# Last full group of 1024 tokens in a fused attention and soft-MoE kernel: its tokens and exponentials turned by TensorE, its slot sums placed behind the last attention sums

## The chip, the core and the metric

The kernel runs on one core of one Trainium2 chip. The metric is the device time of one execution in microseconds (us). The median of three runs of the kernel before is 1390.17 us (1388.31 to 1393.09).

## The reference

An attention without softmax is followed by a soft mixture of experts over all tokens of all batches. B is 8, S is 2496, D is 256, the key width is 64, N = B * S = 19968 tokens, 8 experts with 4 slots each make 32 slots, and F is 1024.

```python
scores = (1 / S) * z @ z.T                    # per batch
x = u * (maximum(scores, 0) ** 2 @ v)         # [N, D], all batches in a row
logits = x @ phi                              # [N, 32]
d = exp(logits - logits.max(0)); d /= d.sum(0) + 1e-9     # over the tokens
slot_input = d.T @ x                          # [32, D]: the slot sums
slot_out = per expert: maximum(slot_input @ w1, 0) @ w2
c = exp(logits - logits.max(1)); c /= c.sum(1) + 1e-9     # over the slots
out = c @ slot_out                            # [N, D]
```

## The kernel before

**Attention.** For each batch the queries go in chunks of up to 512, and for each chunk the 20 key tiles of 128 go in ten *halves* of two tiles. A half needs its squared scores: they are made by TensorE and ScalarE (`scores`, the two activations in `prepare`) or, where the mirrored block was already made, loaded from a turned copy in DRAM (`fetch`, DMA r<-turned). `prepare` splits them into a rounded part `ph` (a cast, mostly by ScalarE) and a rest `pl` (VectorE), and the sums over the keys (PE acc<-ph,v and acc<-pl,v, 12 matmuls for a half of full shape) need both. Past the first dozen halves `prepare(k)` is called three halves ahead of the sums that use it; when a half's scores are made anew, it stands in the middle of the sums of the half three earlier. `ph`, `pl` and `r` have four buffers each, so a cast waits for the sums of four halves earlier. The last chunk of the last batch is cut into two chunks of 256 queries: these are the last twenty halves, here numbered 0 to 19.

**Soft MoE of a group.** When a chunk's sums end, VectorE multiplies them with u into `xg_q`, which holds x of 1024 tokens, turned (features on partitions). `groups(q)` returns a list of small steps, and the main loop takes one step from the list `work` ahead of each half's sums (in the last twenty halves at every half). The steps are: `logits` (TensorE, then VectorE for the running maximum), `exps` (ScalarE), the turning of x and of the exponentials so that tokens lie on partitions, the slot sums (TensorE), adding them to `slot_acc` (`add_up`, VectorE), and the softmax over the slots (`combine`, `combine_exp`, `combine_sum`, `combine_turn`). The lists `middle` and `behind` hold functions that the next `prepare` runs, between its two activations and at its end.

**The turning.** VectorE transposes 32 by 32 blocks (`turn_block` four times, `turn_e` once) into `y`, and `shift` moves the blocks of `y` to their partitions of `xt` with four DMAs each (xt<-y); there are four shifts for a group, 16 DMAs. All DMAs are issued by SyncE (SP), in the order of the program. An instruction there that waits holds up all that follow: the loads of r, of u and of the expert weights w.

**Slot sums.** For a group before the last two, `slot_sums` is run inside the `logits` of the next group. For group 18, the last full one (tokens 18432 to 19455, its second half finished by the chunk that ends just ahead of half 0), there is a schedule of its own in the else branch of `groups`. In the kernel before, two turning steps are taken ahead of the others, `logits` stands at half 5, the shifts at halves 8 to 11, `combine` and its followers at 12 to 15, `slot_sums` at half 16 and `add_up` at 17. The slot sums write the one buffer of the PSUM pool `ms_ps`.

**The tail.** The last 512 tokens (group 19) are treated after the loop: x is multiplied, `logits` of the last group, `exp`, two of the four x tiles turned by TensorE (`turn_x`, tr_last and et_sums; the other two were turned ahead of halves 18 and 19, tr_first), the slot sums of that group (et_sums<-xt), merging of the two maxima, then the expert layers (h, hT, po) and the output (`tokens`: pf by TensorE, ot by ScalarE and VectorE, the store outT by DMA). Ahead of its `logits` stand four transposes without use (`fill(4)`). The weights w of the experts are loaded during the last thirty halves and just behind the loop, into buffers that the attention frees.

Of the kernel before, what the change touches and what calls it, by code (L numbers as in the profile page):

```python
# [8 lines left out]
F32 = mybir.dt.float32  # L9
# [3 lines left out]
ALU = mybir.AluOpType  # L13
# [3 lines left out]
P = 128  # L17
B, S, D, DQK = 8, 2496, 256, 64
N = B * S
E_, SE, FF = 8, 4, 1024  # L20
NS = E_ * SE
# [5 lines left out]
NQG = (NG + 1) // 2  # L27
# [4 lines left out]
NRAW = 4  # L32
# [32 lines left out]
def attn_soft_moe_kernel(ctx, tc, uT, v, zz, phi, ww, outT):  # L65
    nc = tc.nc

    pe, act, dve, sp = (InOrder(tc, x) for x in (nc.tensor, nc.scalar, nc.vector, nc.sync))
# [10 lines left out]
    ms_ps = ms_st.enter_context(tc.tile_pool(name="ms_ps", bufs=1, space=PSUM, side="right"))  # L79
# [3 lines left out]
    raws = moe.enter_context(tc.tile_pool(name="raws", bufs=1))  # L83
# [47 lines left out]
    for p in range(NP):  # L131
        two = [(load_v, 2 * p), (load_v, 2 * p + 1)]
# [13 lines left out]
    ident = cpool.tile([P, P], F32, name="ident")  # L146
# [8 lines left out]
    xt = xpool.tile([P, 4, NB], F32, name="xt")  # L155
    slot_acc = [cpool.tile([P, D + 1], F32, name=f"slot_acc{i}") for i in range(2)]
# [70 lines left out]
    middle, behind, stores = [], [], []  # L227
# [181 lines left out]
    def finish_chunk(b, ch, acc):  # L409
        _, _, n, t0 = ch  # L410
        ut = ut_.pop(t0)
        s = 0
        while s < n:
            q, o = divmod(t0 + s, 1024)
            w = min(n - s, 1024 - o)
            if q not in xg_:
                xg_[q] = wk.tile([P, 2, 1024], F32, tag="xg", name=f"xg_{q}")
            for c in (slice(0, 1), slice(1, 2)) if t0 + n == N else (slice(0, 2),):
                dve.tensor_mul(xg_[q][:, c, o : o + w], acc[:, c, s : s + w], ut[:, c, s : s + w])
            if o + w == 1024:  # L420
                work.extend(todo_.pop(q, None) or groups(q))
            elif q == NQG - 2 and o + w == 512:

                todo_[q] = groups(q)
                work.extend([todo_[q].pop(0) for _ in range(2)])
            s += w

    late, adding, todo_ = [], [], {}


    xt_last = [xt[:, t, 0:D] for t in range(4)]
# [6 lines left out]
    def copy_x(copy, ps, t):  # L438
        copy(
            xt_last[t].rearrange("p (g c f) -> p c g f", c=2, f=32),  # L440
            ps.rearrange("p (c g f) -> p c g f", c=2, f=32),
        )

    def shift(src, a):


        for b in range(4):
            sp.dma_start(xt[32 * b : 32 * b + 32, a], src[32 * a : 32 * a + 32, b])

    def groups(q):  # L450
# [81 lines left out]
        def slot_sums(ps):  # L532
            for j in range(2):
                for t in range(4):
                    o = 2 * D + j * NS
                    for h, rows in enumerate(HALF):
                        pe.matmul(
                            ps[t * NS : (t + 1) * NS, h, 0:D].rearrange("p (g n) -> p g n", g=4),
                            xt[rows, t, o : o + NS],
                            xt[rows, :, j * D + t * 64 : j * D + (t + 1) * 64],  # L540
                            start=(j == 0), stop=(j == 1),
                        )
            (behind if q < NQG - 3 else adding).append(lambda: add_up(ps))

        def add_up(ps):
# [12 lines left out]
            dve.tensor_add(snew[:, 0:D], snew[:, 0:D], ps[:, 1, 0:D])  # L558

        blocks = [lambda j=j, c=c: behind.append(lambda: turn_block(j, c)) for j in range(2) for c in range(2)]  # L560
        shifts = [lambda a=a: shift(y(), a) for a in range(4)]
        e, c0, c2, c3 = (lambda f=f: behind.append(f) for f in (turn_e, combine, combine_sum, combine_turn))
        ex, c1 = (lambda f=f: middle.append(f) for f in (exps, combine_exp))
        rest = lambda: None
        if q < NQG - 2:

            todo = [logits, ex, *blocks, e, shifts[0], c0, shifts[1], c1, shifts[2], c2, shifts[3]]
            todo.append(lambda: (c3(), late.append(slot_sums)))
        else:


            add = lambda: behind.append(adding.pop(0))
            todo = [*blocks[:2], rest, *blocks[2:], rest, logits, ex, e, lambda: (shifts[0](), add()), *shifts[1:]]
            todo += [c0, c1, c2, c3]
            todo.append(lambda: slot_sums(ms_ps.tile([P, 2, 512], F32, tag="ms", name=f"sl_{q}")))
            todo.append(add)
        return todo

    parts = {}
# [50 lines left out]
    work = []  # L630
# [43 lines left out]
    def between_last(k):  # L674

        if k:
            if k == 1:
                xps.append(sc_ps.tile([P, 2, QC], F32, tag="sc", name="tr_first"))
            ps = xps[0][:, k - 1, 0:D]
            turn_x(ps, xg_[NQG - 1], k - 1)  # L680
            copy_x(act.copy, ps, k - 1)

# [22 lines left out]
    for h, x in enumerate(halves):  # L705
# [23 lines left out]
        if x.ends:  # L729
            finish_chunk(x.b, x.ch, acc)  # L730
# [16 lines left out]
    q = NQG - 1  # L747
    x = xg_.pop(q)
    mold, sold = runmax[(q + 1) % 2], slot_acc[(q + 1) % 2]
# [3 lines left out]
    snew = tiny[:, 512 : 512 + D + 1]  # L753
# [6 lines left out]
    E = wk.tile([P, 2 * P], F32, tag="E", name="E_last", bufs=1)[:, 0:P]  # L760
# [18 lines left out]
    def fill(n, ps=ep_):  # L779
# [18 lines left out]
    for t, copy, ps in (2, act.copy, xq[:, 0, 0:D]), (3, dve.tensor_copy, ep_[:, 1, 0:D]):  # L798
        turn_x(ps, x, t)
        copy_x(copy, ps, t)  # L800
# [234 lines left out]
```

## Time and profile before

| | |
|---|---|
| median of three runs | 1390.17 us |
| profiled execution, its time | 1389.86 us |
| span of the profiled execution | 1387.9 us |
| time outside the span (start and end) | 1.96 us |
| TensorE (PE) busy | 1355.0 us, 98% of the span |
| VectorE (DVE) busy | 1083.1 us, 78% |
| ScalarE (ACT) busy | 913.2 us, 66% |
| mean granted TensorE clock | 0.982 |

The profile is of one execution. Its page gives busy times, the span in 40 slices, the chain of work that ended last and the costliest groups of instructions; the trace behind it answers questions on a stretch of time (timeline by engine, windows, waits). Times in the trace are us from the start of the span. Nearly all instructions carry line 61, that of a helper that keeps each engine's program order, so rows are told apart by the names of their tiles: `out<-in`. A row "[5.80 <-DMA xt<-y]" says that the engine sat idle 5.80 us ahead of it, until that transfer ended. Rows of matmuls give lengths that overlap, since matmuls are pipelined; the chain of work gives steps that add up.

### The profile page before, as it was taken

To read this page: it belongs to the slowest core of one execution; us is meant where nothing else is said; L and a number is where in the kernel's file an instruction comes from. 1 tells how busy PE (TensorE), PEld (TensorE's weight loads), DVE (VectorE), ACT (ScalarE), POOL (GpSimd) and SP (SyncE) were. 2 spreads that over 40 slices of the span, in tenths; PEclk is the share of its full clock that TensorE was granted. 3 is DMA by queue.
4 is the path that set the end of the run, shared out by engine and by line. 5 is a ranking of instruction groups with operands and counts; after the bars stand their busy time and mean duration, and the time that the engine had idled before them with its cause. 6 is when DMAs were issued, how large, how long until landed. Compare 5 with 4: busy or idle time off the path is not lost.

```text
span 1387.9 us, 27271 instructions
## 1 busy us (share of the span) xinstructions
PE 1355.0 (98%) x11029; PEld 1074.4 (77%) x11029; DVE 1083.1 (78%) x1401; ACT 913.2 (66%) x1046; POOL 4.2 (0%) x22
## 2 busy tenths in 40 slices
PE   9999999999999999999999999999999999999785
PEld 6777887788777887778877888778877788778652
DVE  6868896779878798579977888687986979676454
ACT  7866786657756687556857677466866677664253
POOL 0000000000000000000000000000000000000000
PEclk9999999999999999999999999999999999999985
DMA  4336567394676747576665755758565856659889
GB/s 130 78 106 184 192 156 198 99 302 149 167 210 213 254 108 184 154 233 211 175 197 137 291 147 135 208 166 292 130 175 167 296 163 166 199 173 330 265 333 387
DMA packets 106493, 272.74 MB, mean 197 GB/s; under 512 B 14720, under 2 KB 17280, under 8 KB 95104
## 3 DMA queue, kind: packets, MB, share of 16 engines
q1 hardware_dynamic: 106368, 271.02, 64.2%
q8 instruction: 86, 1.41, 0.4%
q14 instruction: 39, 0.32, 0.1%
HBM read 148.41 MB, written 100.14 MB: 179 GB/s over the span
## 4 chain that ended last, share of the span: by engine, by line
PE 91%; DMA 3%; ACT 2%; DVE 2%; SPq 1%; issue 1%; ACTq 0%; DVEq 0%
PE acc L61 72%; PE sc L61 12%; PE lg L61 2%; DMA r<-turned 2%; PE pf L61 2%; ACT ot L61 1%; DMA xt<-y 1%; SPq L61 1%; DVE pl L61 1%; PE po L61 1%; ACT r L61 1%; PE h L61 1%; DMA ut<-in_uT 0%; PE idle L61 0%; DVE y L61 0%
## 5 line engine op out<-in xcount | busy, mean ns | idle before, releaser
L61 PE MATMUL acc<-ph,v 64*128 64x512 f32 (+5 forms) x5092 | 986.2, 386 | 0.4 <-DVE v L61 0.4
L61 PEld LDWEIGHTS acc<-ph,v 64*128 64x128 f32 (+1 forms) x5092 | 598.5, 185 | 147.4 <-issue 20.0
L61 DVE TENSOR_TENSOR pl<-r,ph 128x1024 fp32r<-128x1024 f32 (+1 forms) x412 | 487.3, 1189 | 186.5 <-ACT ph L61 172.0
L61 PE MATMUL acc<-pl,v 64*128 64x512 f32 (+5 forms) x2546 | 623.4, 383 | 1.3 <-DVE pl L61 1.1
L61 ACT CAST ph<-r 128x1024 fp32r<-128x1024 f32 (+1 forms) x259 | 261.6, 1021 | 196.8 <-DMA r<-turned 132.3
L61 ACT ACTIVATE r<-sc 128x1024 f32<-128x1024 f32 (+1 forms) x252 | 255.1, 1013 | 188.2 <-PE sc L61 179.4
L61 PEld LDWEIGHTS acc<-pl,v 64*128 64x128 f32 (+1 forms) x2546 | 307.5, 185 | 62.3 <-DVE pl L61 3.9
L61 ACT ACTIVATE r<-r 128x1024 f32<-128x1024 f32 (+1 forms) x252 | 263.5, 1047 | 7.2
L61 DVE STREAM_TRANSPOSE y<-r 128x1024 f32<-128x1024 f32 x152 | 188.2, 1238 | 0.0
L61 PE MATMUL sc<-z,z 64*128 64x512 f32 x960 | 138.6, 393 | 0.9 <-ACT r L61 0.9
L61 DVE CAST ph<-r 128x1024 fp32r<-128x1024 f32 (+1 forms) x153 | 102.0, 667 | 42.2 <-ACT r L61 40.7
L61 PEld LDWEIGHTS sc<-z,z 64*128 64x128 f32 x960 | 89.7, 184 | 23.4 <-ACT r L61 2.2
L61 PE MATMUL sc<-z 64*128 64x512 f32 (+1 forms) x480 | 67.7, 387 | 0.0
L61 DVE TENSOR_TENSOR xg<-acc,ut 128x1024 f32<-128x1024 f32 (+7 forms) x57 | 48.3, 869 | 20.0 <-PE acc L61 20.0
L61 DVE TENSOR_TENSOR v<-vr,v 128x512 fp32r<-128x512 f32 x80 | 54.0, 674 | 3.6 <-ACT v L61 3.6
L61 DVE STREAM_TRANSPOSE y<-xg 128x512 f32<-128x512 f32 x76 | 52.5, 691 | 0.0
L61 PEld LDWEIGHTS sc<-z 64*128 64x128 f32 x480 | 44.4, 184 | 8.7
L61 ACT CAST v<-vr 128x512 fp32r<-128x512 f32 x80 | 48.7, 609 | 2.1 <-DMA vr<-in_v 2.1
L61 DVE TENSOR_TENSOR z<-zr,z 64x512 fp32r<-64x512 f32 x70 | 48.1, 687 | 2.0
L61 ACT CAST z<-zr 64x512 fp32r<-64x512 f32 x70 | 43.4, 620 | 2.0 <-DMA zr<-in_zz 0.3
L61 DVE COPY ot<-pf 128x1024 f32<-128x1024 f32 (+2 forms) x22 | 24.3, 1104 | 21.6 <-PE pf L61 21.6
L61 ACT COPY ot<-pf 128x1024 f32<-128x1024 f32 (+2 forms) x22 | 20.1, 916 | 25.6 <-PE pf L61 25.6
(128 smaller groups left out, 408.1 us busy)
## 6 DMA issues: line engine op xcount, KB each, us to landing
turned<-y SPq DMA_DIRECT2D x304, 256.0 KB, 4.3
r<-turned SPq DMA_DIRECT2D x72, 1024.0 KB, 7.8
xt<-y SPq DMA_DIRECT2D x304, 72.0 KB, 3.4
vr<-in_v SPq DMA_DIRECT2D x80, 256.0 KB, 2.9
w<-in_w SPq DMA_DIRECT2D x32, 512.0 KB, 7.5
outT<-ot SPq DMA_DIRECT2D x16, 1024.0 KB, 6.5
ut<-in_uT SPq DMA_DIRECT2D x31, 512.0 KB, 4.3
zr<-in_zz SPq DMA_DIRECT2D x35, 256.0 KB, 7.7
```

Of the source, the lines that this page charges most:

```text
L61: return lambda *a, **k: self.tc.keep_in_program_order(f(*a, **k))
```

## The change

The change concerns group 18, and what of the tail stands next to it.

- `turn_block`, `turn_e`, the 16 DMAs xt<-y and the early start of two steps are gone for this group; `logits` now stands at half 2, `exps` at 3, the adding of group 17's slot sums at 4, a new `add_counts` (one small VectorE instruction) at 5, and `combine` and its followers at halves 6 to 9.
- At half 10 TensorE turns the exponentials (two transposes, `turn_e_whole`) and ScalarE copies them into `xt`. At halves 11 to 14 TensorE turns x, four transposes at each (`turn_x_whole`), and ScalarE copies each of these with two instructions. All of them go through the one buffer of `ms_ps`.
- The slot sums (`last_slot_sums`) are put on the list `late` and run behind the loop, ahead of the `logits` of the tail, as 8 matmuls over all 128 tokens of a tile instead of 16 over 64 each. One VectorE instruction adds them to `slot_acc`.
- In the tail `fill(4)` is gone; `fill(2)`, which stays, writes a tile of its own; the turned tiles of the last 512 tokens lie in two buffers of the pool `raws` and no longer in `xt`.

```diff
-                work.extend(todo_.pop(q, None) or groups(q))
-            elif q == NQG - 2 and o + w == 512:
-                todo_[q] = groups(q)
-                work.extend([todo_[q].pop(0) for _ in range(2)])
+                work.extend(groups(q))
...
+        def turn_e_whole():
+            ps = ms_ps.tile([P, 2, 512], F32, tag="ms", name=f"et_{q}")
+            for j in range(2):
+                pe.transpose(ps[:, 0, j * P : (j + 1) * P], E()[:, j * P : (j + 1) * P], ident)
+            act.copy(
+                xt[:, :, 2 * D :].rearrange("k t (j s) -> k j t s", s=NS),
+                ps[:, 0, 0 : 2 * P].rearrange("k (j t s) -> k j t s", j=2, s=NS),
+            )
+
+        def turn_x_whole(i):
+            j, t0 = i // 2, i % 2 * 2
+            ps = ms_ps.tile([P, 2, 512], F32, tag="ms", name=f"xt_{q}_{i}")
+            for k in range(2):
+                turn_x(ps[:, k], x, 4 * j + t0 + k)
+            for k in range(2):
+                copy_x(act.copy, ps[:, k, 0:D], xt[:, t0 + k, j * D : (j + 1) * D])
+
+        def last_slot_sums(ps):
+            for j in range(2):
+                for t in range(4):
+                    pe.matmul(
+                        ps[t * NS : (t + 1) * NS, 0, 0:D], xt[:, t, 2 * D + j * NS : 2 * D + (j + 1) * NS],
+                        xt[:, t, j * D : (j + 1) * D], start=(j == 0), stop=(j == 1),
+                    )
+            snew, sold = slot_acc[q % 2], slot_acc[(q + 1) % 2]
+            dve.scalar_tensor_tensor(
+                snew[:, 0:D], sold[:, 0:D], m[:, 3:4], ps[:, 0, 0:D], op0=ALU.mult, op1=ALU.add
+            )
...
-            add = lambda: behind.append(adding.pop(0))
-            todo = [*blocks[:2], rest, *blocks[2:], rest, logits, ex, e, lambda: (shifts[0](), add()), *shifts[1:]]
-            todo += [c0, c1, c2, c3]
-            todo.append(lambda: slot_sums(ms_ps.tile([P, 2, 512], F32, tag="ms", name=f"sl_{q}")))
-            todo.append(add)
+            todo = [rest, rest, logits, ex, lambda: behind.append(adding.pop(0)), lambda: behind.append(add_counts)]
+            todo += [c0, c1, c2, c3, turn_e_whole, *[lambda i=i: turn_x_whole(i) for i in range(4)]]
+            todo.append(lambda: late.append(last_slot_sums))
...
+    late.pop()(ms_ps.tile([P, 2, 512], F32, tag="ms", name="sl_last"))
+
     acc_st.close()
     sc_st.close()
...
-    xq = ms_ps.tile([P, 2, 512], F32, tag="ms", name="tr_last")
+    xq = tp[:, 1, 0:D]
...
-    fill(4)
     logits(0)
     logits(1)
...
-    fill(2, xq)
+    fill(2)
```

On TensorE, at the end of the last sums and the start of the tail, the kernel before has these rows (acc are the sums of half 19, et_sums<-ident the transposes without use, lg_last the logits of the last 512 tokens, the last two the turning of their tiles 2 and 3):

```order
L61 MATMUL acc_15110<-pl_15270,v_5_12649 128x256
L61 MATMUL et_sums<-ident 128x128 x4
L61 MATMUL lg_last<-xg_15108,phi_sb 32x128 x8
L61 MATMUL tr_last<-ident,xg_15108 128x128 x2
L61 MATMUL et_sums<-ident,xg_15108 128x128 x2
```

The changed kernel has at the same place:

```order
L61 MATMUL acc_15106<-pl_15264,v_5_12649 128x256
L61 MATMUL sl_last<-xt 32x256 x8
L61 MATMUL lg_last<-xg_15104,phi_sb 32x128 x8
L61 MATMUL et_last<-ident,xg_15104 128x128 x2
L61 MATMUL et_sums<-ident,xg_15104 128x128 x2
```

The slot sums of group 18 (sl_last) have taken the place of the four transposes without use; before, they stood ahead of the sums of half 16.

On ScalarE, around halves 7 to 13, the kernel before has these rows (ph_15022 to ph_15195 are the casts for halves 10, 11, 14, 15 and 16, r_15082 and r_15126 the two activations each for halves 12 and 13, L the exponentials of the softmax over the slots):

```order
L61 CAST ph_15022<-r_14867 128x2x256
L61 CAST ph_15044<-r_14867 128x2x256
L61 ACTIVATE r_15082<-sc_15083 128x2x256
L61 ACTIVATE r_15082<-r_15082 128x2x256
L61 ACTIVATE r_15126<-sc_15127 128x2x256
L61 ACTIVATE r_15126<-r_15126 128x2x256
L61 CAST ph_15155<-r_15019 128x2x256
L61 CAST ph_15174<-r_15019 128x2x256
L61 ACTIVATE L_14937<-L_14937 128x256
L61 CAST ph_15195<-r_15063 128x2x256
```

The changed kernel has there (casts for halves 10, 11, 14 and 15, activations for 12 and 13):

```order
L61 ACTIVATE L_14880<-L_14880 128x256
L61 CAST ph_15025<-r_14903 128x2x256
L61 CAST ph_15042<-r_14903 128x2x256
L61 ACTIVATE r_15077<-sc_15078 128x2x256
L61 ACTIVATE r_15077<-r_15077 128x2x256
L61 COPY xt<-et_15107 128x2x4x32
L61 ACTIVATE r_15122<-sc_15123 128x2x256
L61 ACTIVATE r_15122<-r_15122 128x2x256
L61 COPY xt<-xt_0_15147 128x2x4x32 x2
L61 CAST ph_15154<-r_15021 128x2x256
L61 COPY xt<-xt_1_15173 128x2x4x32 x2
L61 CAST ph_15180<-r_15021 128x2x256
```

The exponentials L have moved ahead of the casts for halves 10 and 11, and the copies of the turned tiles stand between the activations and casts.

More of the change, by code (lines that the diff above doesn't have):

```diff
@@ L420, in finish_chunk @@
             if o + w == 1024:
-                work.extend(todo_.pop(q, None) or groups(q))
-            elif q == NQG - 2 and o + w == 512:
-                todo_[q] = groups(q)
-                work.extend([todo_[q].pop(0) for _ in range(2)])
+                work.extend(groups(q))
             s += w
-    late, adding, todo_ = [], [], {}
-    xt_last = [xt[:, t, 0:D] for t in range(4)]
+    late, adding = [], []
+    xt_last = []
     def turn_x(ps, x, t):
@@ L436, in turn_x, with copy_x @@
             pe.transpose(ps[:, c * P : (c + 1) * P], x[:, c, t * P : (t + 1) * P], ident)
-    def copy_x(copy, ps, t):
+    def copy_x(copy, ps, to):
         copy(
-            xt_last[t].rearrange("p (g c f) -> p c g f", c=2, f=32),
+            to.rearrange("p (g c f) -> p c g f", c=2, f=32),
             ps.rearrange("p (c g f) -> p c g f", c=2, f=32),
@@ L543, in slot_sums, with add_counts @@
             (behind if q < NQG - 3 else adding).append(lambda: add_up(ps))
+        def turn_e_whole():
[24 more added lines that the diff above has]
+            )
+        def add_counts():
+            snew, sold = slot_acc[q % 2], slot_acc[(q + 1) % 2]
+            dve.scalar_tensor_tensor(
+                snew[:, D : D + 1], sold[:, D : D + 1], m[:, 3:4], m[:, 4:5], op0=ALU.mult, op1=ALU.add
+            )
         def add_up(ps):
@@ L678, in between_last @@
                 xps.append(sc_ps.tile([P, 2, QC], F32, tag="sc", name="tr_first"))
+                two = [raws.tile([P, 2, D], F32, tag="raw", name=f"xt_last_{i}", bufs=NRAW) for i in range(2)]
+                xt_last.extend(t[:, i] for t in two for i in range(2))
             ps = xps[0][:, k - 1, 0:D]
             turn_x(ps, xg_[NQG - 1], k - 1)
-            copy_x(act.copy, ps, k - 1)
+            copy_x(act.copy, ps, xt_last[k - 1])
     dve.memset(cw[:, 0:2], 0.0)
@@ L775, in attn_soft_moe_kernel, with fill @@
     pm = sc_ps.tile([P, QC], F32, tag=sc_ps.name, name="pm")
-    xq = ms_ps.tile([P, 2, 512], F32, tag="ms", name="tr_last")
     tp, ep_ = (acc_ps.tile([P, 2, QC], F32, tag=acc_ps.name, name=n) for n in ("et_last", "et_sums"))
-    def fill(n, ps=ep_):
+    xq = tp[:, 1, 0:D]
+    def fill(n):
+        ps = ms_ps.tile([P, 2, 512], F32, tag="ms", name="fill")
         for _ in range(n):
@@ L797, in attn_soft_moe_kernel @@
     act.activation(E, lg[:, 0:P], AF.Exp, bias=mneg[:, 0:1], accum_out=snew[:, D : D + 1])
-    for t, copy, ps in (2, act.copy, xq[:, 0, 0:D]), (3, dve.tensor_copy, ep_[:, 1, 0:D]):
+    for t, copy, ps in (2, act.copy, xq), (3, dve.tensor_copy, ep_[:, 1, 0:D]):
         turn_x(ps, x, t)
-        copy_x(copy, ps, t)
+        copy_x(copy, ps, xt_last[t])
     pe.matmul(pm[:, 0:P], mall.to_broadcast([P, P]), ident, start=True, stop=True)
```

## Prediction

> **What bounds the kernel now.** I read the page first, then windows over the last 120 us, then the timeline of each engine and the chain of work there.
>
> ```profile
> span 1387.9 us, 27271 instructions
> PEclk9999999999999999999999999999999999999985
> PE 91%; DMA 3%; ACT 2%; DVE 2%; SPq 1%; issue 1%; ACTq 0%; DVEq 0%
> ```
>
> TensorE carries the chain. Work taken from VectorE or DMA therefore pays only where TensorE waits for it, and work added to TensorE is paid in full. The windows find the one place with such a wait (columns: us; busy time of PE, PEld, DVE, ACT, POOL; granted clock; DMA share; GB/s):
>
> ```profile
> 1296.00:1302.00 6.00, 0.20 (x2) 0.16 (x2) 2.48 (x7) 1.14 (x2) 0.00 (x0) 0.93 1.01 269
> 1306.00:1308.00 2.00, 2.00 (x11) 2.00 (x11) 0.00 (x0) 0.00 (x0) 0.00 (x0) 0.51 1.00 397
> 1308.00:1310.00 2.00, 2.00 (x19) 2.00 (x18) 0.00 (x0) 0.38 (x1) 0.00 (x0) 1.00 1.02 406
> 1318.00:1326.00 8.00, 8.00 (x71) 2.69 (x72) 6.75 (x12) 5.78 (x9) 0.00 (x0) 1.00 1.02 411
> ```
>
> From 1296 to 1302 TensorE does nearly nothing, and up to 1308 it runs at a granted clock of 0.51. TensorE's timeline names the cause:
>
> ```profile
> 1286.92 0.40 PE L61 MATMUL acc<-ph,v 64*128 64x256 f32 x4
> ...
> 1295.79 0.28 PE L61 MATMUL acc<-pl,v 128*128 128x256 f32 x1
> 1301.87 2.25 PE L61 MATMUL sl<-xt 64*32 64x256 f32 x32 [5.80 <-DMA xt<-y]
> 1304.05 0.79 PE L61 MATMUL acc<-ph,v 128*128 128x256 f32 x2
> ...
> 1308.03 0.40 PE L61 MATMUL acc<-ph,v 128*128 128x256 f32 x2
> ```
>
> The slot sums of group 18 wait 5.80 us for the last shift. SP's timeline shows why it comes late: the 16 issues take about 0.6 us each and stand among loads that wait as well.
>
> ```profile
> 1289.05 4.95 SPq L61 DMA_DIRECT2D xt<-y  x8
> 1294.11 0.53 SPq L61 DMA_DIRECT2D r<-turned  x1
> ...
> 1295.19 2.41 SPq L61 DMA_DIRECT2D xt<-y  x4
> ...
> 1298.33 22.19 SPq L61 DMA_DIRECT2D w<-in_w  x20
> ```
>
> The chain of work, whose steps add up, prices everything from there on:
>
> ```profile
> 1301.87 2.25 PE sl L61 x32
> 1304.12 4.78 PE acc L61 x24
> 1308.90 0.22 PE tr_first L61 x2
> 1309.12 1.42 PE acc L61 x12
> ...
> 1312.20 0.76 DVE xg L61 x2
> ...
> 1313.10 0.63 PE et_sums L61 x4
> 1313.73 0.57 PE lg_last L61 x16
> ...
> 1315.90 0.62 PE et_sums L61 x8
> ...
> 1320.47 5.29 PE h L61 x48
> 1325.76 1.90 PE hT L61 x16
> ```
>
> **The change, part by part.** *Removed from TensorE's path.* (1) The wait, 5.80 us. (2) The slot sums at half 16, 2.25 us. (3) The slow stretch behind the wait: 24 matmuls took 4.78 us, 12 at full clock take 1.42, so 4.78 - 2 x 1.42 = 1.94 us. Together 9.99 us.
>
> *Added to it.* 18 transposes of 128 by 128, two at half 10 and four each at halves 11 to 14. Two of the same kind (tr_first) take 0.22 us in the chain, 16 in a row (hT) 1.90, so 0.11 to 0.12 each: 18 x 0.11 = 1.98 us, at most 2.14.
>
> The Trainium skill speaks against this part: its page "TensorE: Matmul & The Clock Gate", section "Part 4: PE-mode transpose", puts a transpose at about 275 ns in a kernel and says that transposes do not count as activity that lifts the clock. By that figure the 18 would take 4.95 us and the gain would be about 3 us smaller; here such matmuls overlap, so the chain's 0.11 us holds for the sum, and hT ran at clock 1.00 (the window from 1318).
>
> *The slot sums, moved to the tail.* They are now 8 matmuls of 128 by 32 with 256 columns, the shape of et_sums x8, which is four of them in two passes each: 0.62 us, so 1.24 us for eight. They need only `xt` and a PSUM bank that has long been free, so they start when half 19's sums end. There TensorE was idle in any case while VectorE multiplied x (1312.20 to 1312.96), and then ran the four useless transposes, so lg_last began 1.53 us behind the start of that multiplication. Now it begins 1.24 us behind the sums: 0.3 us gained. VectorE's new addition to `slot_acc` comes between, and queued behind it is the maximum of lg_last, on which the exponentials wait:
>
> ```profile
> 1304.21 0.48 DVE L61 SCALAR_TENSOR_TENSOR slot_acc<-slot_acc,m,sl 128x256 f32<-128x256 f32 x1 [3.10 <-PE sl L61]
> ```
>
> It takes 0.48 us and runs beside lg_last (0.57 us), so it costs nothing; without that cover it would cost 0.48.
>
> *Moved earlier.* The logits go from half 5 to half 2, their matmuls unchanged. VectorE loses four transposes of x and one of the exponentials, all beside TensorE's work: no gain by themselves. But the softmax over the slots moves from half 12 to half 6, and there it meets a tight place:
>
> ```profile
> 1284.26 1.29 DVE L61 TENSOR_TENSOR pl<-r,ph 128x512 fp32r<-128x512 f32 x2
> ...
> 1292.10 0.44 DVE L61 STREAM_TRANSPOSE L<-L 128x256 f32<-128x256 f32 x1
> 1292.57 0.42 DVE L61 TENSOR_REDUCE rm<-L 128x8 f32<-128x256 f32 x1
> 1293.03 0.43 DVE L61 TENSOR_TENSOR L<-L,rm 128x256 f32<-128x256 f32 x1
> ```
>
> ```profile
> 1282.49 0.50 ACT L61 ACTIVATE E<-L,m 128x256 f32<-128x256 f32 x1
> ...
> 1283.07 0.62 ACT L61 ACTIVATE r<-r 128x512 f32<-128x512 f32 x1
> ...
> 1293.49 0.42 ACT L61 ACTIVATE L<-L 128x256 f32<-128x256 f32 x1 [2.48 <-DVE L L61]
> 1298.84 1.14 ACT L61 CAST ph<-r 128x512 fp32r<-128x512 f32 x2 [3.90 <-DMA r<-turned]
> 1309.15 0.38 ACT L61 COPY xt<-tr_first 128x256 f32<-128x256 f32 x1 [9.18 <-PE tr_first L61]
> ```
>
> ScalarE's exponentials L now wait for the three VectorE steps (1.36 us from 1292.10 to 1293.46), and the casts for halves 10 and 11, which followed the square at 1283.07, queue behind them. VectorE can start these steps when `pl` for half 9 is done. That was at 1284.26 + 1.29 / 2 = 1284.9, and it comes 0.58 us earlier, since the exponentials E (1282.49 to 1283.07) no longer stand ahead of the square for half 9: 1284.3. Then L is ready at 1285.7; the casts begin some 0.35 us behind and take 1.14 us for two, so `ph` for half 10 is there at 1286.6 and for half 11 at 1287.2. Half 10 begins at 1286.92 as before, since nothing ahead of it on TensorE grows, and it now starts with two transposes: its cast is in time by 0.4 us, its `pl` (0.65 us more) by about nothing. Next ScalarE has the two activations for half 12 (2 x 0.62) and the copy of the turned exponentials (0.38), until 1288.8. Half 11 begins at 1286.92 + 1.88 (1288.80 before, by the same timeline) + 0.22 = 1289.0, and its four transposes need the bank that this copy frees. From then on ScalarE has two copies and a cast for each half, 0.76 + 0.57 = 1.33 us, while TensorE has 1.42 + 0.44 = 1.86: it catches up, but at half 12, where the activations for half 13 still stand ahead of the copies, it may be late by 0.1 us. I charge 0.25 us for these small waits, with bounds of 0 and 1.0 us (the second if ScalarE or VectorE runs 0.5 us later at two of the places).
>
> *Queues.* SP loses 16 issues. The load of r for half 18 was issued at 1294.11 and landed at 1298.84, where the cast stopped waiting: 4.7 us. Now it waits only for `pl` of half 15, whose buffer it takes. Half 12 begins at 1290.9; its transposes, two copies, the cast for half 15 and the subtraction put that at 1290.9 + 0.44 + 0.76 + 0.57 + 0.65 = 1293.3, up to 1293.9 with VectorE's softmax steps in the queue. So r lands by 1298.6, its cast is done by 1299.2, and half 18 begins at about 1300.6: hidden, with 1.4 us to spare, and that is the price if TensorE ran that much earlier. Behind it on SP stand u and the expert weights w. The w began in earnest at 1298.33 and now follow r, 3 us earlier, while TensorE comes 8 us earlier, so their cover shrinks. Up to the last w of layer 1 that is waited for (w11) there are eleven w of 512 KB, r and u, 6.3 MB: at 411 GB/s 15.3 us from about 1295.6 on, so 1311, or 1313 with a landing time of 1 to 2 us. It is needed in the middle of h x48, at 1320.47 + 2.6 - 8.1 = 1315. Hidden, by 2 us.
>
> *The end.* The output is limited by its stores:
>
> ```profile
> 1360.00:1370.00 10.00, 6.62 (x49) 3.38 (x50) 5.35 (x5) 4.45 (x5) 0.00 (x0) 0.50 1.02 419
> ```
>
> Stores start when the first output tile is ready, so this stage moves forward as a whole and keeps its length.
>
> *Sum.* 9.99 - 1.98 - 0.25 + 0.30 = 8.06 us gained. The profiled execution took 1389.86 us, 0.31 below the median of the runs: 1389.86 - 8.06 = 1381.8 us.
>
> **The rivals.** A measurement of this kernel can tell about 0.3% (4.2 us) from no change; the three runs before spread over 4.8 us.
>
> *Forecast* (chance 0.78): as above. With the bounds of the small waits and of the transposes, and runs that spread by 2 us either way, 1379 to 1384.5 us.
>
> *The handshake binds* (0.11). TensorE turns, ScalarE copies and casts, VectorE subtracts, and TensorE's next transposes wait for the one bank. If the copies come behind casts that wait for sums, each of the five steps stands for a copy and a cast more, 0.4 to 0.9 us: 2 to 4.5 us lost, 1384 to 1386.3 us. For it: the margins of 0 to 0.4 us above. Against: `prepare` runs three halves ahead.
>
> *Weights or r come late* (0.06). If loads land 3 us later than reckoned, layer 1 waits 1 us, and if half 18 waits for r, up to 2 us more: 1383 to 1385. For it: the DMA share of 1.00 to 1.02 from 1306 on. Against: the covers of 1.4 and 2 us reckoned above.
>
> *The clock does not hold, slower* (0.03). The transposes, without sums between them for 0.45 us in each of halves 11 to 14, let the granted clock fall to 0.50, and it stays there to the end of half 19. At half clock 18 matmuls took from 1304.05 to 1308.03, 0.22 us each instead of 1.42 / 12 = 0.118, so 1.24 us more a half: nine halves cost 11.2 us, and the transposes twice their price 2 us more: 8.06 - 13.2 = -5.1, so 1395 us. It decides from seven halves at half clock on. The Trainium skill's sentence that transposes do not count as activity, in the section named above, would lead here. Against: tr_first stood among sums at clock 1.00, and 16 transposes in a row did not lower it.
>
> *No change* (0.02). The wait might only move, to another load that the shifts had covered, so that 5 us or more of the gain are given back: 1387 to 1391. The order of instructions speaks against it: no xt<-y of group 18 is left.
>
> **How the numbers follow.** The likeliest case gives 1381.8 us. The range runs from 1378.8 (no small waits, a low run) to 1386.0 (most of the handshake and of late loads), and leaves out the slow clock, the no-change case and the far end of the handshake, under 2 in 10. Faster by over 0.3% (below 1386.0): 0.78 and most of the two partial cases, 0.90. Within 0.3%: 0.06. Slower: 0.04.
>
> **What would show it.** In the profile of the changed kernel: no xt<-y DMA behind 1285 us, and no wait of TensorE over 1 us between half 10 and the tail; granted clock 1.00 in every window from 1284 to about 1330; et and xt_0 to xt_3 rows stepping 0.11 us each; sl_last x16 beginning within 0.1 us of the last acc, and lg_last some 1.3 us behind; the sums of half 19 ending near 1304 instead of 1312.2, the first store some 8 us earlier. I am wrong if TensorE waits for ScalarE's copies at halves 11 to 14, for r at half 18, for w in layer 1, if the clock drops, or if the output stage grows by what was gained.

## The result, and the profile after

| | before | after |
|---|---|---|
| median, us | 1390.09 (1388.31 to 1393.09, 4 runs) | 1382.27 (1381.62 to 1384.49, 4 runs) |
| profiled execution, its time | 1389.86 | 1381.88 |
| span | 1387.9 | 1380.1 |
| mean granted clock | 0.982 | 0.985 |

The ratio of after to before is 0.9948, with a 95% interval of 0.9936 to 0.9961: 7.8 us less. The forecast was 1381.8.

The windows of after over the stretch in which the kernel before stood still and then ran at half clock (columns as in the prediction):

```profile
1290.00:1296.00 6.00, 6.00 (x54) 6.00 (x53) 4.61 (x8) 4.04 (x11) 0.13 (x1) 1.00 0.64 207
1296.00:1302.00 6.00, 6.00 (x54) 6.00 (x53) 2.08 (x3) 2.58 (x6) 0.67 (x2) 1.00 1.03 411
1302.00:1308.00 6.00, 5.77 (x68) 4.43 (x69) 2.65 (x10) 1.50 (x7) 0.00 (x0) 1.00 1.03 412
```

TensorE is busy all through but for 0.23 us, at clock 1.00. The chain of work of after prices the new steps and the tail:

```profile
1287.68 0.37 PE et L61 x2
...
1289.68 0.59 PE xt L61 x4
1290.27 1.41 PE acc L61 x12
1291.68 0.44 PE xt L61 x4
...
1295.81 5.61 PE acc L61 x48
1301.42 0.22 PE tr_first L61 x2
...
1304.67 1.04 PE sl_last L61 x16
...
1310.06 1.92 PE h L61 x16
...
1312.55 5.29 PE h L61 x48
```

Four transposes among sums of 128 rows add 0.44 us, the matmuls between them keep their 1.41, and the slot sums follow the last sums at once. The two at half 10 and the first four, at half 11, have 0.37 and 0.59: there the rows of the matmuls change shape, which is priced below. SP's timeline of after shows what the 16 DMAs leave behind:

```profile
1290.73 0.33 SPq L61 DMA_DIRECT2D r<-turned  x1
...
1292.11 21.94 SPq L61 DMA_DIRECT2D w<-in_w  x20
```

The r of half 18 left at 1290.73 (before: 1294.11), the weights from 1292.11 on (before: 1298.33).

### The profile page after: what moved, and what is told of

The parts are those of the page before. It is cut to its first block, busy times and chain, and to the rows that moved or that the text cites. A ratio compares the mean times of both kernels' runs of the same rounds, so it can differ in the third digit from the quotient of the medians.

```text
span 1380.1 us, 27240 instructions
## 1 busy us (share of the span) xinstructions
PE 1353.3 (98%) x11027; PEld 1074.0 (78%) x11027; DVE 1080.8 (78%) x1395; ACT 916.2 (66%) x1055; POOL 3.8 (0%) x22
## 3 DMA queue, kind: packets, MB, share of 16 engines
q8 instruction: 86, 1.41, 0.4%
## 4 chain that ended last, share of the span: by engine, by line
PE 89%; DMA 4%; ACT 3%; DVE 2%; issue 1%; SPq 1%; ACTq 0%; DVEq 0%
PE acc L61 71%; PE sc L61 12%; DMA r<-turned 3%; PE lg L61 3%; PE pf L61 1%; ACT ot L61 1%; ACT r L61 1%; DMA zr<-in_zz 1%; DVE pl L61 1%; SPq L61 1%; ACT ph L61 1%; PE po L61 1%; PE h L61 1%; DMA outT<-ot 0%; DMA ut<-in_uT 0%
## 5 line engine op out<-in xcount | busy, mean ns | idle before, releaser
L61 DVE STREAM_TRANSPOSE y<-xg 128x512 f32<-128x512 f32 x72 | 49.7, 690 | 0.0
```

The lines of the kernel that those rows point to most:

```text
L61: return lambda *a, **k: self.tc.keep_in_program_order(f(*a, **k))
```

## The experiments

The theory at first was that of the prediction: the gain is the removed wait with its half clock, less the transposes. The rival was that the gain comes from SP's queue, where the shifts held up r, u and w. Ratios are to the kernel before, run beside each. The profile of a kernel is of one execution, and executions differ already ahead of the change: where the logits of group 18 stand at half 2, they begin between 1272.61 and 1275.87 us. A difference in time between two traces holds only to that extent; before and after run level (half 0 begins at 1269.99 and 1270.02 us).

### late_only: the slot sums alone are moved

The kernel before, still turning by VectorE and DMA, with the slot sums behind the last sums and the tail of the changed kernel.

```diff
-            todo.append(lambda: slot_sums(ms_ps.tile(...)))
-            todo.append(add)
+            todo += [..., lambda: late.append(slot_sums)]
...
+    late.pop()(ms_ps.tile([P, 2, 512], F32, tag="ms", name="sl_last"))
+    adding.pop(0)()
```

> Blocks turned by VectorE and 16 shift DMAs as in the kernel before, at the same halves; only the slot sums of group 18 are moved behind the last sums. Theory (the loss was TensorE standing at half 16 for the last shift, 5.8 us, and the slow clock behind it, so any place behind the landing of that shift is as good): no wait for xt<-y, no transposes of group 18 on TensorE (2.0 to 2.3 us less than the changed kernel), but r for half 18 and the weights stay behind the shifts on SP, about 1 us of wait at half 18: 1381 us, between 1380 and 1382.5. Rival (the turning by TensorE is what brings the gain, since the shifts on SP hold up r and w): the wait moves to half 18 and to layer 1, 3 us or more, 1384 to 1389 us.

1386.31 us (1384.01 to 1388.21, 7 runs), ratio 0.9967 [0.9955, 0.9979]: about half of the gain, as the rival said. (The profiled execution, at 1388.21, is the slowest of the seven.) The wait at half 16 is gone and another stands at half 18. Its chain of work:

```profile
1296.74 5.56 DMA r<-turned
...
1302.41 0.63 ACT ph L61
...
1303.81 2.45 PE acc L61 x10
...
1314.28 3.52 PE h L61 x16
```

TensorE's timeline has the wait as 1.37 us for `ph` and 0.23 for `pl`:

```profile
1303.08 0.50 PE L61 MATMUL acc<-ph,v 128*128 128x256 f32 x2 [1.37 <-ACT ph L61]
1303.81 0.53 PE L61 MATMUL acc<-pl,v 128*128 128x256 f32 x1 [0.23 <-DVE pl L61]
```

Ten matmuls then took 2.45 us, where 12 take 1.41, and the first 16 of h 3.52 instead of 1.92. Its windows show why:

```profile
1304.00:1307.00 3.00, 3.00 (x15) 3.00 (x16) 0.68 (x2) 0.28 (x1) 0.00 (x0) 0.50 1.04 319
...
1315.00:1317.00 2.00, 2.00 (x16) 0.39 (x8) 0.78 (x3) 0.75 (x1) 0.00 (x0) 0.50 1.02 408
```

A wait of 1.6 us was followed by some 3 us at a granted clock of 0.50, and the short gaps of the tail by another stretch. SP's own waits in this kernel say where r was held:

```profile
SPq L61 <- DVE y L61: 6.2, 1, 6.2
```

The first shift waits 6.2 us at the head of the queue for VectorE's turned blocks, with both late r behind it; the r of half 18 also has twelve issues of shifts ahead of it.

### early_dma_late: the same, with the shifts two halves earlier

```diff
-            todo = [*blocks[:2], rest, *blocks[2:], rest, logits, ex, e, lambda: (shifts[0](), add()), *shifts[1:]]
+            todo = [*blocks[:2], lambda: (blocks[2](), blocks[3]()), logits, ex, lambda: (e(), add())]
+            todo += [lambda: (shifts[0](), behind.append(add_counts)), *shifts[1:]]
+            todo += [c0, c1, c2, c3, lambda: late.append(slot_sums)]
```

> As late_only, and the steps of group 18 stand earlier: logits at half 2, shifts at halves 6 to 9, the softmax over the slots at 10 to 13. Theory: no wait for xt<-y, shifts issued by about 1290 so that r for half 18 is in time, no transposes on TensorE: 1390.1 - 10.0 - 0.4 + 0.4 (two VectorE additions in the tail) = 1380 us, about 2 us faster than the changed kernel. Rival (SP held up by 16 issues costs what the transposes cost): 1382.3 us or more.

1389.34 us (1387.45 to 1390.98, 12 runs), ratio 0.9993 [0.9984, 1.0002]: nothing gained. TensorE's timeline, its chain of work from there, and SP's timeline:

```profile
1302.06 0.80 PE L61 MATMUL acc<-ph,v 128*128 128x256 f32 x2 [3.79 <-ACT ph L61]
```

```profile
1302.06 5.73 PE acc L61 x24
1307.78 0.22 PE tr_first L61 x2
```

```profile
1292.23 3.83 SPq L61 DMA_DIRECT2D xt<-y  x4
1296.17 1.00 SPq L61 DMA_DIRECT2D r<-turned  x2
```

Now both late r leave behind the last shift, and it is half 16 that waits, 3.79 us for its cast: two halves, 24 matmuls, follow before the transposes that stand ahead of half 18. The clock from 1302 to 1308 is 0.54. Moving the shifts made the wait longer and brought it back to half 16.

### turn_only: TensorE turns, the slot sums stay at half 16

```diff
-            todo.append(lambda: late.append(last_slot_sums))
+            todo.append(rest)
+            todo.append(lambda: last_slot_sums(ms_ps.tile(...)))
...
+    fill(4)
```

VectorE's addition of these sums goes to the end of the next `prepare` (`behind`).

> The changed kernel with the slot sums of group 18 put back at half 16 and the four useless transposes put back in the tail. Theory: turning by TensorE alone removes the wait; the slot sums cost 1.04 us in the loop and the tail is as long as before (0.4 us more): 1383.7 us. Rival (the place behind the last sums carries the gain): 1388 us or more, with a wait at half 16.

1383.12 us (1382.64 to 1383.96, 5 runs), ratio 0.9948 [0.9936, 0.996]. Most of the gain is there without the late slot sums; in the chain they follow the sums with no wait:

```profile
1298.93 0.35 PE acc L61 x3
1299.28 1.00 PE sl L61 x16
```

So of the two halves of the change, the turning by TensorE carries it. The place of the slot sums adds 1.0 us by the rows, which the times do not separate: from the logits at half 2 to hT it is 45.85 us here (1273.65 to 1319.50) and 44.85 in after (1272.98 to 1317.83).

### turn_x4: each transpose four times

```diff
-            for j in range(2):
+            for j in [0, 1] * 4:
...
-            for k in range(2):
+            for k in [0, 1] * 4:
```

> The changed kernel with every transpose of group 18 issued four times, 72 in place of 18. Theory (0.11 us each in the stream, clock unchanged): 54 x 0.11 = 6.0 us more, 1388.3 us, granted clock 1.00 through halves 10 to 15. Rival by the Trainium skill, TensorE: Matmul & The Clock Gate, Part 4 (275 ns each, and transposes do not hold the clock up): 54 x 0.275 = 14.9 us more, 1397 us, and a granted clock of 0.50 in halves 11 to 15, where transposes are more than half of the work.

1388.07 us (1386.66 to 1390.73, 10 runs), ratio 0.9985 [0.9975, 0.9995]. A step of the chain, and one window over the bursts:

```profile
1293.74 1.75 PE xt L61 x16
```

```profile
1290.00:1299.00 9.00, 9.00 (x85) 8.87 (x82) 4.03 (x7) 3.87 (x10) 0.00 (x0) 1.00 0.78 269
```

Twelve transposes more in a step cost 1.75 - 0.44 = 1.31 us, 0.109 each, at clock 1.00.

### wait_turns and wait_turns66: the wait of before filled with transposes

The kernel before, with 46 or 66 transposes of the identity ahead of the slot sums at half 16.

```diff
+            for _ in range(66):
+                pe.transpose(ps[:, 1, D : D + P], ident, ident)
+            slot_sums(ps)
```

> The kernel before with 46 transposes of the identity, read by nobody, put on TensorE at half 16 ahead of the slot sums, so that it works through the 5.8 us in which it waited. Theory (transposes keep the granted clock up as matmuls do): clock 1.00 from 1296 to 1308, slot sums 1.0 us and the matmuls behind them at their full pace: about 3.1 us less than the kernel before, 1387 us. Rival (transposes don't count for the clock): the clock falls to about 0.5 as before and 1390 us, or up to 1392.

> The kernel before with 66 transposes of the identity ahead of the slot sums at half 16, where 46 left TensorE idle for 2.25 us. Theory (a gap of over a microsecond or two lets the clock fall, and transposes hold it): no gap, clock 1.00 through 1296 to 1310, slot sums in 1.0 us, the matmuls behind them at full pace; the wait stays, filled: 2 to 3 us less than the kernel before, 1387 us. Rival (transposes do not hold the clock): half clock behind them as before, 1390 us.

With 46: 1389.72 us (1387.67 to 1391.56, 10 runs), ratio 0.9998 [0.9989, 1.0007]. They took 5.19 us, TensorE still waited 2.25, and then the clock fell. TensorE's timeline and its window behind the wait:

```profile
1295.62 5.19 PE L61 MATMUL sl<-ident 128*128 128x128 f32 x46
1303.06 2.42 PE L61 MATMUL sl<-xt 64*32 64x256 f32 x32 [2.25 <-DMA xt<-y]
```

```profile
1303.00:1306.00 3.00, 2.94 (x34) 1.55 (x35) 0.43 (x2) 0.00 (x0) 0.00 (x0) 0.50 1.03 405
```

With 66: 1389.12 us (1387.82 to 1390.66, 10 runs), ratio 0.9994 [0.9985, 1.0004]. The same views:

```profile
1296.11 7.37 PE L61 MATMUL sl<-ident 128*128 128x128 f32 x66
1303.40 1.09 PE L61 MATMUL sl<-xt 64*32 64x256 f32 x32
```

```profile
1296.00:1299.00 3.00, 3.00 (x30) 3.00 (x29) 1.06 (x4) 0.00 (x0) 0.00 (x0) 1.00 0.95 308
...
1302.00:1305.00 3.00, 3.00 (x51) 2.30 (x49) 0.39 (x1) 0.00 (x0) 0.00 (x0) 1.00 0.99 390
```

7.37 us of transposes alone kept the clock at 1.00, and the slot sums took 1.09 us instead of 2.25. The time that I expected of it (1387) did not come: the slot sums began 1.53 us later than in the profile of before (1303.40 against 1301.87), which gives back half of the 3 us: 66 transposes take 7.37 us, and the wait that they fill was 5.80. On the clock the verdict rests on these rows; the time by itself is within the interval of no change.

The Trainium skill's page "TensorE: Matmul & The Clock Gate", section "Part 4: PE-mode transpose", gives about 275 ns for one in a kernel and says that the full clock doesn't engage for it. Here the row of a single transpose is about that long (0.30 us for et_last<-ident,E_last in before), but in a stream each adds 0.109 us, and the clock held through 7.37 us of them; the measurement decides.

### after_spload and after_spwait: sixteen copies put back on SP

The changed kernel, with 16 small copies that nobody reads at the shifts' old places; in the second kernel the first four also wait, for a `pl`.

```diff
+        def shift_e(a):
+            late_pl = pend[max(pend)][1]
+            for b in range(4):
+                src = f32(late_pl...) if a == 0 else E()     # after_spload: E() for all
+                sp.dma_start(y()[32 * b : 32 * b + 32, a, 0 : 2 * P], src[32 * a : 32 * a + 32, 0 : 2 * P])
```

> The changed kernel with sixteen small copies put back on SyncE's queue at the places where the kernel before had its shifts (four ahead of the r of half 16, eight between it and the r of half 18, four behind that); they carry a part of E that nobody reads, and TensorE turns x as in the changed kernel. Theory of the queue (the sixteen issues of 0.6 us, and their wait for what they carry, hold up r and the weights): the r of half 18 is issued at about 1294.3 instead of 1290.7 and lands at about 1300, with a cast and a difference behind it, so half 18 (1301.4) starts at the time or up to 1.5 us late; the weights for the last layers come 5 to 6 us later; 1384 to 1387 us. Rival, the account of the prediction (only the wait at half 16 and what went with it was removed): 1382.3 us, as the changed kernel, within 0.7.

> The changed kernel with the sixteen small copies on SyncE's queue, of which the first four now also wait, as the shifts did for y: they read the pl of a half that is two ahead. In the run without this wait the queue had them done early and the r of half 18 left at 1292.4 (changed kernel: 1290.7), and nothing was lost. Theory (it is the wait at the head of the queue that makes r late, more than the issues): the r of half 18 leaves at 1294.5 or later and lands at 1300 or later, with 1.3 us of cast and difference behind it; half 18 (1301.4) waits 0 to 1.5 us, and where it waits over a microsecond TensorE falls to half clock for 3.3 us: 1383 to 1386 us, with a wait of acc for ph at half 18. Rival (r has slack still): no wait, 1382.3 to 1383.6 us.

after_spload: 1383.59 us (1381.97 to 1386.01, 4 runs), ratio 0.9958 [0.9943, 0.9974]; its profile has a span of 1380.2, like that of after, and no wait of TensorE for r. SP's timeline:

```profile
1280.31 3.39 SPq L61 DMA_DIRECT2D y<-E  x4
...
1285.68 6.62 SPq L61 DMA_DIRECT2D y<-E  x8
1292.40 0.52 SPq L61 DMA_DIRECT2D r<-turned  x1
```

The issues alone made r 1.7 us later, and that was covered. My expectation of 1384 to 1387 was too dear: its median lies just below, its profile well below. after_spwait: 1387.73 us (1386.09 to 1390.68, 11 runs), ratio 0.9984 [0.9975, 0.9992], slower than expected. SP's timeline and TensorE's:

```profile
1291.08 2.41 SPq L61 DMA_DIRECT2D y<-pl  x4
...
1300.14 0.52 SPq L61 DMA_DIRECT2D r<-turned  x1
```

```profile
1305.33 0.50 PE L61 MATMUL acc<-ph,v 128*128 128x256 f32 x2 [0.94 <-ACT ph L61]
```

A wait at the head of the queue brings back the wait of half 18 (0.94 us, and 0.23 for `pl`), although nothing of TensorE's or VectorE's work was moved. The price is more than that wait. Against the profile of after, half 16 begins 2.75 us later (1301.20), as late as the logits at half 2 were already, and the slot sums begin 4.46 us later (1309.06), so half 18 costs 1.7 us. The tail up to h is as long as in after, but then the chain has

```profile
1314.51 3.56 PE h L61 x16
```

where after has 1.92, at a granted clock of 0.50 from 1315 to 1317: 1.6 us more. The copy also waited longer than the shift of before did (8.1 against 6.7 us). So the mechanism is shown, but not what the shifts of the kernel before cost in this way.

### late_r_gp: late_only with r issued by GpSimd

```diff
-        sp.dma_start(
+        queue = gp if k >= len(halves) - 4 else sp
+        queue.dma_start(
             r.rearrange("p a j r -> p a (j r)"), scratch[x.b, x.p, j][:, a0 : a0 + na]
```

> The kernel before with its slot sums of the last full group behind the last sums (1386.3 us, the first experiment), and with the last two loads of r (for halves 16 and 18) issued by GpSimd and not by SyncE, so that the shifts no longer stand ahead of them; the shifts stay on SyncE, and x is turned by VectorE and DMA. Theory (r behind the shifts in the queue made half 18 wait, and TensorE's stretch at half clock behind that wait came of it): no wait at half 18, no slow stretch behind it, 1.6 + 1.6 us less than the first experiment, 1383 us; if the slow first layer goes too, 1381.5 us, under the changed kernel since no transposes are paid. Rival (the weights behind the shifts, or VectorE's extra work, cost the time, and not r): 1385.5 to 1387 us.

1383.50 us (1383.02 to 1385.40, 5 runs), ratio 0.9956 [0.9944, 0.9969]: 6.5 us under the kernel before beside it, where late_only was 4.4 under its own, and level with the changed kernel without a transpose in the chunk. The intervals of the two overlap; the rows decide. Half 18 no longer waits; the granted clock is 1.00 in every window from 1284 to 1320. The next thing that stood behind the shifts now ends the chain:

```profile
1307.37 10.56 DMA w<-in_w
...
1317.97 2.77 PE h L61 x20
```

From the first row of h, at 1309.92, to its end at 1320.74 it is 10.8 us; after needs 1317.84 - 1310.06 = 7.8 (1312.55 + 5.29 is that end). So the late weights give back 3 us, somewhat more than the missing transposes save.

The Trainium skill's page "DMA: Bandwidth & Descriptors", section "Issuing engines are not separate DMA queues", says that a second issuing engine saves only the time of the issue, usually small. Here the issue of an r is 0.3 to 0.7 us, and more than that was saved: the r of half 18 no longer stood behind a shift that waited and behind the issues of twelve shifts, and left at 1291.81 instead of 1296.74.

### early_gp and early_rw_gp: the early turning, with shifts or loads moved to GpSimd

Both start from early_dma_late, which early_gp's expectation calls the third experiment. early_gp issues the shifts by GpSimd; early_rw_gp issues two r and eight w by GpSimd and leaves the shifts on SP.

```diff
-        shifts = [lambda a=a: shift(y(), a) for a in range(4)]
+        shifts = [lambda a=a: shift(y(), a, sp if q < NQG - 2 else gp) for a in range(4)]     # early_gp
...
-            load_w(k)
+            load_w(k, gp if 23 <= i < 30 else sp)                                             # early_rw_gp
```

> The kernel of the third experiment of this study that turned x early by VectorE and DMA and took its slot sums behind the last sums (1389.3 us), with the sixteen shifts issued by GpSimd, which has nothing to do there, and not by SyncE. No transposes on TensorE in the chunk. Theory of the queue: r and the weights are issued as early as in the changed kernel, there is no wait at half 18 and no slow stretch; the 18 transposes (2.0 us) are saved: about 1380.3 us (1379.5 to 1381.5). Rival (VectorE, the blocks that it turns and their buffers hold up the powers, not SyncE): 1386 to 1390 us. Second rival (an issue of GpSimd takes so long that the shifts come behind the last sums): 1383 us or more, with a wait of the slot sums for xt.

> The kernel that turned x early by VectorE and DMA, with its slot sums behind the last sums (1389.3 us, the second experiment), with the loads of r for halves 16 and 18 and eight of the last weights issued by GpSimd; the shifts stay on SyncE, and TensorE turns nothing in the chunk. When r alone left SyncE, half 18 no longer waited, but the first layer waited for weights that came behind the shifts, and its end was 2.8 us later than in the changed kernel against its start. Theory (r and the weights behind the shifts are the whole price of turning by DMA): no wait for r at half 18 and none for w in the first layer, and the 2.0 us of transposes saved: 1380 to 1381.5 us, under the changed kernel. Rival (the transfers, which fill the DMA engines, and not the order of a queue, make the weights late): h waits for w as before, 1383 to 1384 us.

early_gp: 1390.56 us (1388.89 to 1394.02, 10 runs, the slowest of them profiled), ratio 1.0007 [0.9998, 1.0016]. I had said that GpSimd has nothing to do there; it has. In `sums_halves` the first phase of the sums hands over to the second through an empty GpSimd instruction, and this now stood behind shifts that waited. TensorE's waits:

```profile
PE acc L61 <- POOLq L386: 6.4, 2, 4.6
```

It tells nothing of SP's queue. early_rw_gp: 1390.64 us (1385.68 to 1394.96, 12 runs), ratio 1.0 [0.9987, 1.0013]. Neither r nor w is waited for long any more, and u, which finishes the last chunk, is. TensorE's timeline, SP's, and the chain of work:

```profile
1309.13 0.79 PE L61 MATMUL lg_last<-xg,phi_sb 128*32 128x128 f32 x12 [4.44 <-DVE xg L61]
```

```profile
1290.98 4.84 SPq L61 DMA_DIRECT2D xt<-y  x4
```

```profile
1296.54 12.02 DMA ut<-in_uT
```

So my expectation failed again at the same point, a load that I had not looked at, but not by the queue alone. u left behind the last shifts, at 1296.54; in the kernel before it left later still, at 1297.70, and landed in 5.1 us, in time. Here it took 12.0 us, while an r and eight w issued by GpSimd were on their way too. So the rival of this expectation, that the transfers and not the order of a queue make a load late, fails for w and fits u; that GpSimd's loads were what slowed u was not tested apart. The runs of this kernel spread over 9 us and the profiled one (1386.7) is near the fast end; what the slower ones add is open.

### after_tail: the tail's two small waits

```diff
-    xq = tp[:, 1, 0:D]
+    xq = sl_last[:, 1, 0:D]
...
     dve.tensor_tensor(mall, mneg[:, 0:1], mneg[:, 1:2], op=ALU.min)
+    add_last()
```

> The changed kernel with two edits behind the last sums: x of the last tile but one is turned into the free half of the tile of the last slot sums and not into the tile of E's transpose, so that E's transpose doesn't wait for ScalarE's copy (0.26 us), and VectorE adds the slot sums behind the maxima of the last logits (0.1 us ahead of the last exponentials). Theory (both waits lie on the chain that ends last): 0.3 us less than the changed kernel, about 1382.0 us. Rival (the row that then waits is the copy of E, and nothing is gained): 1382.3 us. Below what these runs can tell by time, so the rows of E_last, et_last and h decide.

1383.21 us (1381.89 to 1383.87, 5 runs), ratio 0.9947 [0.9935, 0.996]: nothing gained. The edit made a new wait, in TensorE's waits:

```profile
PE sl_last L61 <- DVE slot_acc L61: 1.0, 1, 1.0
```

The transposes of x now wait until VectorE has read the slot sums from the same tile. From the start of sl_last to h it took 5.87 us (1306.14 to 1312.01), in after 5.39.

## Why the prediction was right, and where it was not

The time was right (1381.8 against 1382.27). Of its terms the largest was, and so, by luck, was that of the small waits; the transposes cost 0.32 us more than reckoned, and the tail gained 0.15 more. The table's measured numbers are differences between rows of the two traces, from the end of one row to the end of another.

| step | predicted, us | measured, us |
|---|---|---|
| wait, slot sums and slow stretch removed | 9.99 | 10.02 |
| 18 transposes | -1.98 | -2.30 |
| small waits, halves 0 to 9 | -0.25 | -0.24 |
| tail | +0.30 | +0.45 |
| sum | 8.06 | 7.93 |

The first: from the end of half 15 to the end of half 17 it took 12.83 us in before (1296.07, where the row at 1295.79 ends, to 1308.90) and takes 2.81 in after (1298.61, where the row at 1298.33 ends, to 1301.42). The second: from the end of half 9 to that of half 15, 8.63 in before (from 1287.44) and 10.93 in after (from 1287.68). TensorE's rows around half 10, of before and of after:

```profile
1287.16 0.28 PE L61 MATMUL acc<-pl,v 64*128 64x256 f32 x2
1287.27 0.40 PE L61 MATMUL acc<-ph,v 64*128 64x256 f32 x4
...
1288.80 0.50 PE L61 MATMUL acc<-ph,v 128*128 128x256 f32 x2
```

```profile
1287.40 0.28 PE L61 MATMUL acc<-pl,v 64*128 64x256 f32 x2
1287.61 0.44 PE L61 MATMUL et<-ident,E 128*128 128x128 f32 x2
...
1289.61 0.66 PE L61 MATMUL xt<-ident,xg 128*128 128x128 f32 x4
...
1298.33 0.28 PE L61 MATMUL acc<-pl,v 128*128 128x256 f32 x1
```

- **The transposes** cost more than their upper bound of 2.14. Nearly all of the excess stands at half 10, where two transposes of 128 rows stand between sums of 64 rows: from the last row ahead of half 10 to the start of half 11 it is 1.64 us in before and 2.21 in after, 0.57 more, where the prediction had 0.22. The step from 64 rows to 128 is 0.21 us (1287.40 to 1287.61), where rows of one shape have 0.11 (1287.16 to 1287.27). That the change of shape is the cause was not tested apart.
- **The handshake** had slack. No matmul of halves 10 to 15 waited for a copy or a cast. The prediction took 1286.92 for the start of half 10; it is 1287.27, so every margin there was 0.35 us larger than reckoned. That the 0.25 us charged for it came out as 0.24 is luck: these were lost ahead of half 10, where nothing was charged. The logits, of 64 rows, now stand among sums of 128 rows, which makes two changes of shape more, of about 0.1 us each.
- **SP's queue** is the step that failed. The prediction had r for half 18 wait until 1293.3 to 1293.9 for `pl` of half 15 and so leave hardly earlier than before. It left at 1290.73, right behind `pl` of half 12 (VectorE's row ends at 1290.67), so it takes a buffer that half 12 gives up. Before, the shifts had held it to 1294.11. Half 18 was covered either way, so the time came out right. The weights' cover was reckoned with 6.3 MB; twelve loads of 512 KB and one of 256, at 1024 bytes, are 6.55, 0.6 us more of the 2 us of cover. No wait of TensorE for w showed.
- **The deeper error** was to price the removed DMAs at nothing, and to call the wait at half 16 the one cost of turning by DMA. late_only and early_dma_late, which by that account should have reached 1381 and 1380, took 1386.31 and 1389.34. The wait came back at what stood behind the shifts, r in both, and with r out of the way at w (late_r_gp); that it then came back at u (early_rw_gp) was the length of a transfer more than its place. In the changed kernel this could not be seen, since both parts went together; only the rival "No change" had named the mechanism, and for this change the reason given against it held.
- **The tail** gained more than said, 0.45. The slot sums took 1.04 us there and not 1.24, and from the end of the last sums to the last exponentials it is 1.84 us instead of 2.52. Some 0.26 us are given back where E's transpose shares a tile with x and waits for ScalarE's copy. after_tail could not get that back.
- **The clock** held, in after, with four times the transposes, and with 7.37 us of nothing else.

A kernel faster than the changed one was not found. late_r_gp is level with it, with its weights late; a version with r, w and u all ahead of the shifts and on one queue was not run.

## What to carry to other kernels

When a wait on a DMA is taken away by moving its consumer, look at what stands behind that DMA in its issuer's queue. Here the wait moved there, first to r and then to w, and all of it went away only with the turning by DMA itself. What matters is when the loads behind leave, against when they are needed: sixteen issues that were done early delayed r by 1.7 us and cost nothing in the profiled execution, and sixteen of which the first waited 8.1 us brought the wait of half 18 back. A load that leaves in time can still land late, as u did. Ahead of using an idle engine as another queue, look for hand-overs that run through it.

## What the runs showed of the hardware

- Transposes keep the granted clock at 1.00: 66 in a row for 7.37 us, at 0.11 us each.
- A gap of 1.6 us on TensorE was followed by about 3 us at clock 0.50 (late_only), and one of 2.25 us likewise (wait_turns). In the gap of 5.8 us (before) the clock fell ahead of the gap's end: in windows of 1 us it is 1.00 up to 1301, 0.58 from 1301 to 1302, and 0.50 or 0.51 from there to 1308. Gaps of 0.94 and 0.23 us (after_spwait) left it at 1.00 up to 1314.
- In late_only and after_spwait gaps of a few tenths in the tail were followed by half clock too, while the tail of after, with similar gaps, kept 1.00.
- An SP issue of a 72 KB shift took 0.6 us, of a load of r 0.3 to 0.5; u took 5.1 us from issue to landing in before and 12.0 in early_rw_gp.
